# Another set of ranks and not-before times for a fixed list of operations, in a sliding-window attention followed by a token and channel mixer

## The chip, the core and the metric

The kernel runs as one launch on one core of a Trainium2 chip. The metric is the device time of that core in microseconds, as the median of several executions. Before the change three executions took 273.97, 274.58 and 275.58 us, so the median is 274.58 us. The profile is one further execution with the hardware profiler on.

The engines are named as in the profile: PE is the matrix engine (PEld its weight loads, which overlap its matmuls), DVE the vector engine, ACT the scalar engine, POOL the general engine that here issues most loads, and SP the engine that here only issues transfers. Each takes its own instructions strictly in the order in which the program has them, and waits where an operand isn't ready.

## What is computed

```python
def _attn_ref(q, k, v):                     # 8 batches, 8 heads, 576 rows, 64 wide
    scores = scale * np.matmul(q, k.transpose(0, 1, 3, 2))
    mask = (rel >= 0) & (rel < window)      # window = 128
    scores = np.where(mask, scores + bias[None], -1000000000.0)
    attn = np.exp(scores - max) ; attn = attn / (sum + 1e-09)
    return np.matmul(attn, v)

def _moe_ref(x, w_tok1, w_tok2, w_ch1, w_ch2):   # x: 8 x 576 x 512
    h = np.maximum(x.transpose(0, 2, 1) @ w_tok1, 0.0) @ w_tok2
    u = x + h.transpose(0, 2, 1)
    h2 = np.maximum(u @ w_ch1, 0.0) @ w_ch2
    return u + h2
```

The head outputs are laid side by side and become x. Each of the eight batches goes through attention, then through the token mixer (which mixes rows), then through the channel mixer (512 to 1536 and back).

## The kernel before

Two batches form a pair; their 576 rows are cut into eight blocks of 128 rows and one TAIL block that holds the last 64 rows of both. For a block the stages are: loads of q, k and v (POOL, line 614); a transposition of q and k into a tile qkT, for the first blocks on PE (L772) with a copy from PSUM on DVE or ACT (L778, L787), for the later ones as a transfer from SP (L761); scores on PE (L809, and L855 for a shared block), which use half of the rows of the array; exponentials on ACT (L824) and masks on DVE (L834); values on PE (L897), then reciprocal and normalisation (L910, L913, or L919 on ACT), which write the tile xb.

The token mixer of a batch multiplies xb by W1 (L944, with the tail rows in L954), applies a relu (L962 or L963), multiplies by W2 block by block (L987, and L983 for the TAIL block, which uses half of the columns), and DVE adds x (L1005), which writes the tile ub. From batch 3 on SP transposes each block of ub by a transfer (L1013) into uT, or uTt for TAIL; before that PE does it (L1022, L1291). The channel mixer of the batch then multiplies by WC1. In four of the batches some of that is written as seven smaller products of half-blocks (L1402, with DVE preparing differences in tt at L1365, copies at L1417/L1418, sums at L1426 and relus at L1428/L1430); elsewhere it is plain (L1502, relu at L1508 or L1509). TAIL pieces are L1545 with the relu at L1550. The second matrix WC2 is always seven half-block products (L1679), fed by sums on DVE (L1527), and evicted with an addition at L1650; the finished quarter goes to memory from SP or POOL (L1662). The TAIL rows go through L1590 and L1597, and their store is L1606.

The channel mixer of batch b and the attention and token mixer of batch b+1 are interleaved on PE. None of this order is written by hand. Each step is entered in a list (1486 operations, numbered in the order in which they are entered) with an engine, a cost, a rank, what it needs and which buffers it makes. A planner (`Plan.run`) then goes through model time: on each engine, among the operations whose needs are met, the earliest one is taken, and among several that could start at once the one with the lowest rank:

```python
key = (t if t > free[e] + 1e-6 else free[e], own, o.n)
```

PSUM banks and other rings are handed out in the same pass. Some operations may go to either of two engines (DVE or ACT), and the planner settles that too; where it leaves a hole on PE in the first 60 us of its own time it puts in small matmuls on a tile of zeros (L1737). The finished order is then written out engine by engine. POOL alone has an order of its own (`o.order`), which ranks don't touch.

What steers the order beside the costs is a string of triples, NUDGES (line 389). Each names an operation by number, an amount that is added to its rank, and a model time before which it may not start (0 for none):

```python
for item in NUDGES.split():
    n, rank, after = item.split(":")
    ops[int(n)].rank += float(rank)
    ops[int(n)].after = max(ops[int(n)].after, float(after))
```

Of the kernel before, what the change touches and what calls it, by code (L numbers as in the profile page):

```python
# [71 lines left out]
class Plan:  # L72
# [60 lines left out]
    def run(self):  # L133
        ops = self.ops
        for item in NUDGES.split():
            n, rank, after = item.split(":")
# [189 lines left out]
    def emit(self, spin):  # L326
# [20 lines left out]
        for _, _, go in sorted(work, key=lambda w: w[:2]):  # L347
# [41 lines left out]
NUDGES = ("611:-21079:100923 615:-377:0 618:6245:106227 624:11583:0 628:-3532:0 631:-20512:118175 632:4405:0 "  # L389
          "635:13739:113529 638:-6964:114135 641:43614:0 643:-19605:120680 648:13951:125840 652:20901:132489 "  # L390
          "656:1592:130617 662:-3783:94988 668:12595:102360 672:0:99525 676:-4021:0 691:3986:0 694:4455:102094 "
          "706:-16795:109525 710:11799:0 717:5009:114541 723:-30772:115527 725:-13156:0 727:1700:0 731:-799:113884 "
          "737:-15688:124087 742:88:126037 747:-10649:132061 750:-29110.6:133561.55 752:1864:0 753:7662:141715 "
          "756:18322:0 757:13696:0 758:5979:130815 759:2748:0 760:-6228:0 761:25117:132703 763:-2147:0 765:-1777:134943 "
          "766:12861:138150 769:4570:135329 774:-3476:0 778:14785:0 780:7181:136913 782:6347:136777 796:5332:0 799:9009:0 "
          "801:8201:142134 808:2736:0 813:9918:154475 818:-1109:0 820:-5330:154387 833:-4650:0 835:34387:124325 "
          "837:-15506:120235 843:8673:0 857:-16826:126349 858:1715:130121 859:24976:132690 862:8001:133653 "
          "869:22770:125235 870:11407:127731 885:3734:139098 891:9282:135579 895:-4722:0 906:6597:0 929:-1024:0 "
          "934:1522:0 937:4392:0 939:-1560:0 942:20915:0 948:771:175554 950:-4529:179605 951:995:176861 980:-2682:165866 "
          "981:-2735:0 983:1098:0 989:-8428:0 992:-4728:0 995:4194:0 1000:4211:156722 1005:3799:169472 1010:-2057:164371 "  # L400
          "1013:-4825:0 1019:7261:0 1032:-2615:175960 1038:-4243:0 1044:-3493:182549 1047:-1700:185338 1048:8146:185482 "
          "1054:3724:185348 1056:2724:0 1068:-1298:0 1070:3393:0 1074:20899:194114 1077:45251:0 1080:18007:0 "
          "1081:-2386:195024 1087:458:209375 1088:1:199812 1091:-1643:199488 1097:-2044:205608 1111:2214:211061 "
          "1114:17600:0 1119:-16086:212462 1121:-6088:0 1124:52293:0 1133:0:215904 1147:208:186538 1149:1234:0 "
          "1154:3339:0 1163:6504:0 1166:5025:0 1173:-13218:195991 1174:-7990:194582 1175:11221:198039 1181:18370:199015 "
          "1189:-770:198395 1195:5140:0 1201:243:206584 1202:-5634:204124 1213:15048:0 1219:1629:209744 "
          "1232:-23729:221022 1233:-4369:0 1235:2272:0 1237:-12249:0 1238:-11167:221075 1240:4249:0 1241:4209:0 "
          "1242:7504:0 1255:5295:0 1256:0:234956 1257:14642:0 1258:12581:0 1260:3619:0 1262:4895:0 1264:11531:232963 "
          "1267:-4292:227279 1276:5714:238024 1280:962:0 1283:-2021:240378 1288:-141:235787 1290:-9906:246722 "
# [1362 lines left out]
```

## Time and profile before

| | |
|---|---|
| median of three executions | 274.58 us (273.97, 274.58, 275.58) |
| profiled execution, first to last instruction (span) | 272.2 us |
| median less span | 2.4 us |
| granted PE clock over the span | 1.000 |
| PE busy | 263.6 us, 97% |
| PE weight loads busy | 191.8 us, 70% |
| DVE busy | 224.7 us, 83% |
| ACT busy | 150.7 us, 55% |
| POOL busy | 114.7 us, 42% |

The profiled execution has no time of its own on record beside its span; what lies around the span in an ordinary execution (the launch, the last store's completion) can only be taken as the difference to the median, 2.4 us, if that execution was a middling one. Busy times count the engines' own instructions. A PE matmul's end is modelled, so consecutive matmuls overlap in the record, and what a stretch of them takes is read from start to start.

### The profile page before, as it was taken

The page shows a single profiled execution, that of the slowest core. Times are in us where ns is not written, and L with a number is a line of the kernel's source. Part 1 is how long each engine was busy: PE and PEld are TensorE (multiplying, and loading weights), DVE is VectorE, ACT ScalarE, POOL GpSimd, SP SyncE. Part 2 cuts the span into 40 slices and gives each one's busy share as a digit, 9 for nine tenths or more (in the row PEclk, how much of TensorE's full clock was granted, in tenths as well). Part 3 has the DMA queues.
Part 4 walks back from the last instruction along what each step waited for, and adds up shares of the span by engine and source line. Part 5 has one row for each costly group of instructions (what it writes and reads, how often), then busy time and mean ns, then how long its engine had stood idle before and what let it go on. Part 6 is the DMA issues. An engine that isn't in the chain of part 4 may idle for free.

```text
span 272.2 us, 7391 instructions
## 1 busy us (share of the span) xinstructions
PE 263.6 (97%) x2965; PEld 191.8 (70%) x2992; DVE 224.7 (83%) x520; ACT 150.7 (55%) x267; POOL 114.7 (42%) x147
## 2 busy tenths in 40 slices
PE   7989999999999999999999999999999999999994
PEld 5767566676686655587786756498886758589883
DVE  7887699978897569688999478698998989976983
ACT  6973796226881298107992089308973089506700
POOL 8978796840397007800870307800651050004000
PEclk9999999999999999999999999999999999999999
DMA  8999999999999979999999999999999580035005
GB/s 201 178 173 180 167 148 183 157 156 175 186 127 161 192 162 78 137 119 210 200 149 119 142 228 96 140 154 142 212 132 67 110 239 2 2 82 171 4 10 183
DMA packets 160338, 38.59 MB, mean 142 GB/s; under 512 B 146544, under 2 KB 159472, under 8 KB 160304
## 3 DMA queue, kind: packets, MB, share of 16 engines
q0 software_dynamic: 109968, 19.64, 89.4%
q1 hardware_dynamic: 49104, 17.70, 33.4%
q10 hardware_dynamic: 1232, 0.79, 1.0%
q8 instruction: 23, 0.38, 0.5%
q14 instruction: 11, 0.09, 0.1%
HBM read 35.85 MB, written 9.44 MB: 166 GB/s over the span
## 4 chain that ended last, share of the span: by engine, by line
PE 90%; DMA 3%; POOL 3%; issue 1%; ACT 1%; DVE 0%; POOLq 0%
PE ps L1679 27%; PE ps L1502 15%; PE ps L1402 12%; PE ps L897 6%; PE ps L809 5%; PE ps L987 4%; PE ps L944 4%; PE ps L1545 4%; PE ps L1590 4%; DMA W<-in_moe_w_tok_dram 2%; POOL v L623 1%; DMA qkT<-qk 1%; POOL qk L630 1%; PE ps L772 1%; PE ps L1488 1%
## 5 line engine op out<-in xcount | busy, mean ns | idle before, releaser
L614 POOL DMA_DIRECT2D v<-in_v_dram x36 | 30.5, 849 | 76.4 <-PE ps L897 72.8
L824 ACT ACTIVATE pe<-ps 128x1024 bf16<-128x1024 f32 (+1 forms) x56 | 51.3, 969 | 3.1 <-PE ps L809 3.0
L1502 PE MATMUL ps<-uT,WC 128*128 128x512 bf16 x182 | 46.0, 379 | 0.7 <-issue 0.2
L1508 ACT ACTIVATE r<-ps 128x512 bf16<-128x512 f32 x45 | 26.4, 601 | 35.9 <-PE ps L1502 33.8
L1679 PEld LDWEIGHTS <-r 128*128 128x128 bf16 x384 | 36.8, 98 | 7.4 <-issue 0.7
L1679 PEld LDWEIGHTS <-s 128*128 128x128 bf16 x288 | 27.8, 98 | 5.8 <-DVE s L1527 0.4
L614 POOL DMA_DIRECT2D qk<-in_k_dram x35 | 30.3, 873 | 3.7 <-DMA qk<-in_k_dram 1.6
L834 DVE TENSOR_TENSOR pe<-pe,mask 128x1024 bf16<-128x1024 bf16 (+1 forms) x48 | 30.5, 650 | 1.6 <-ACT pe L824 1.4
L614 POOL DMA_DIRECT2D qk<-in_q_dram x35 | 30.2, 867 | 3.7 <-DMA qkT<-qk 1.7
L1502 PEld LDWEIGHTS <-WC 128*128 128x128 bf16 x196 | 17.7, 98 | 18.1 <-issue 0.5
L1417 ACT COPY raw<-ps 128x512 f32<-128x512 f32 x27 | 15.5, 597 | 22.6 <-PE ps L1402 22.6
L1679 PE MATMUL ps<-WC,r 128*128 128x256 bf16 x192 | 24.9, 273 | 0.0
L1679 PE MATMUL ps<-WT,s 128*128 128x256 bf16 x192 | 24.7, 273 | 0.0
L1679 PE MATMUL ps<-WT,r 128*128 128x256 bf16 x192 | 23.8, 273 | 0.1
L897 PEld LDWEIGHTS <-pe 128*128 128x128 bf16 (+1 forms) x480 | 19.5, 99 | 5.6 <-DVE pe L834 0.8
L1426 DVE TENSOR_TENSOR r<-ps,raw 128x512 bf16<-128x512 f32 x30 | 20.2, 680 | 3.3 <-ACT raw L1417 2.8
L897 PE MATMUL ps<-v,pe 128*128 128x65 bf16 (+1 forms) x480 | 22.8, 194 | 0.1
L1005 DVE TENSOR_TENSOR ub<-ps,xb 128x512 bf16<-128x512 f32 x32 | 20.5, 683 | 2.7 <-ACT r L1508 0.9
L913 DVE TENSOR_TENSOR xb<-ps,rt 128x256 bf16<-128x256 f32 (+1 forms) x52 | 21.4, 417 | 0.5
L1650 DVE TENSOR_TENSOR raw<-ps,ub 128x512 f32<-128x512 f32 x25 | 17.0, 686 | 5.8 <-PE ps L1679 5.8
L1402 PE MATMUL ps<-tt,WS 128*128 128x256 bf16 x132 | 18.8, 273 | 0.1
L809 PEld LDWEIGHTS <-qkT 64*128 64x128 bf16 x448 | 11.9, 94 | 8.3 <-issue 5.9
(143 smaller groups left out, 479.4 us busy)
## 6 DMA issues: line engine op xcount, KB each, us to landing
out_dram<-raw SPq DMA_DIRECT2D x19, 256.0 KB, 4.4
qk<-in_q_dram POOLq DMA_DIRECT2D x30, 128.0 KB, 5.4
qk<-in_k_dram POOLq DMA_DIRECT2D x30, 128.0 KB, 5.4
v<-in_v_dram POOLq DMA_DIRECT2D x28, 128.0 KB, 5.1
WC<-in_moe_w_ch_dram POOLq DMA_DIRECT2D x8, 384.0 KB, 7.5
out_dram<-raw POOLq DMA_DIRECT2D x6, 256.0 KB, 3.4
out_dram<-ob SPq DMA_DIRECT2D x5, 256.0 KB, 4.1
v<-in_v_dram POOLq DMA_DIRECT2D x16, 64.0 KB, 4.8
```

The source lines that it names most:

```text
L614: nc.gpsimd.dma_start(out=to()[p0 : p0 + n, :, :], in_=rows(src, b, s0, n))
L809: pe_.matmul(wide(e)[:, i, kind, a:z], lhsT=ts[kb]()[e * D : (e + 1) * D, NHP + i, :], rhs=ts[blk]()[e * D : (e + 1) * D, i, a:z], start=T ...
L824: act_.activation(out=pb()[:, e, :, lo:, c0:c1_], in_=wide(e)[:, :, lo:, c0:c1_], func=ACT.Exp, scale=scale)
L834: dve_.tensor_tensor(out=o, in0=o, in1=heads(mk, es), op=ALU.mult)
L897: pe_.matmul(view()[a:z, at, i, :], lhsT=pb()[:, e, i, kind, a:z], rhs=vb()[:, h, 0 : D + 1], start=m == 0, stop=m == len(mms) - 1, skip_g ...
L913: dve_.tensor_tensor(out=x4(), in0=view()[r0:r1_, :, :, 0:D], in1=rt()[r0:r1_, 0:n, :, :].broadcast_to([r1_ - r0, n, 4, D]), op=ALU.mult)
L1005: plan.op("DVE", 690, lambda blk=blk, ht=ht, hs=hs: dve_.tensor_tensor(out=ub()[:, blk, :], in0=ht()[:, hs], in1=xb()[:, blk, :], op=ALU.a ...
L1402: pe_.matmul(bk()[:, c * HS : (c + 1) * HS], lhsT=l(c, cb), rhs=r(cb), start=new and c == 0 and cb == 0, stop=cb == 1, skip_group_check=True)
L1426: add = plan.op("DVE", 690, lambda: dve_.tensor_tensor(out=o(), in0=half_of(bk), in1=half_of(e), op=ALU.add), rk + UNIT_RANK, uses=[bk, e] ...
L1502: pe_.matmul(ct()[:, :], lhsT=WC1[:, cb, t * P : (t + 1) * P], rhs=uT()[:, cb, :], start=cb == 0, stop=cb == NCB - 1)
L1508: plan.op("ACT", 600, lambda t=t, ct=ct: act_.activation(out=r2()[:, t, :], in_=ct()[:, :], func=ACT.Relu), rk, part=(r2, t), uses=[ct], o ...
L1679: pe_.matmul(bk()[:, c * HN : (c + 1) * HN], lhsT=l(t, c), rhs=w(t), start=first, stop=g == 1 and t == HK - 1, skip_group_check=True)
```

## The change

The string NUDGES is replaced; no other line differs. It had 178 triples, the lowest operation 611 and the highest 1457, and 97 of them with a not-before time. It now has 206 triples, from operation 156 to 1479, and 100 with a not-before time. 78 operations are in both, and none of these keeps its two numbers. The new set was picked by the mean end over scattered transfer and engine times of a fixed order.

```diff
-NUDGES = ("611:-21079:100923 615:-377:0 618:6245:106227 624:11583:0 628:-3532:0 631:-20512:118175 632:4405:0 "
...
-          "1431:-2423:252435 1443:3256:263701 1444:354:262085 1457:-151:263359 ")
+NUDGES = ("156:-15687:54632 159:42592:0 161:18891:0 169:9713:0 293:10443:0 295:-38081:0 303:13240:0 305:29272:0 "
...
+          "1429:-101737:0 1432:-54653:0 1479:50983:0")
```

The same operations are done. What moves is their order on PE, DVE, ACT and SP, the engine of 43 either-or operations (21 go from ACT to DVE and 22 from DVE to ACT), and the number of zero matmuls of L1737 (52 before, 56 now). The order of POOL is unchanged. Line numbers of the changed kernel are 7 higher from NUDGES on. Three places follow.

**PE, batch 0's channel mixer with the first blocks of batch 1.** The rows run from the last transposition of a block of q and k to the first scores that read the transposed tile qkT_83. Before:

```order
L772 MATMUL ps<-ident,qk_71 128x128
L1488 LDWEIGHTS WC_124
L1488 MATMUL ps<-uT_98,WC_124 128x512
L897 LDWEIGHTS pe_86
L897 MATMUL ps<-v_72,pe_86 128x65
...
L1502 LDWEIGHTS WC_124
L1502 MATMUL ps<-uT_98,WC_124 128x512
...
L809 LDWEIGHTS qkT_83
L809 MATMUL ps<-qkT_83 128x128
```

With the change:

```order
L779 MATMUL ps<-ident,qk_71 128x128
L1495 LDWEIGHTS WC_124
L1495 MATMUL ps<-uT_98,WC_124 128x512
...
L1744 LDWEIGHTS zero
L1744 MATMUL ps<-zero 128x128
...
L816 LDWEIGHTS qkT_83
L816 MATMUL ps<-qkT_83 128x128
```

One L1488, four L897 and four L1502 stood between the two; now three of the first kind and three zero matmuls do, and eight value matmuls come behind the scores.

**SP, the end of batch 3's token mixer.** uT_99 and uTt_100 are the transposed tiles of batch 3, qkT_78 and qkT_83 the next blocks for scores of batch 4. Before:

```order
L1606 DMA out_dram<-raw_105 64x512 x2
L1013 DMA_TRANSPOSE uTt_100<-ub_93 128x4x128
L1013 DMA_TRANSPOSE uT_99<-ub_93 128x4x128 x4
L761 DMA_TRANSPOSE qkT_78<-qk_69 128x8x128
L761 DMA_TRANSPOSE qkT_83<-qk_71 128x8x128
```

With the change:

```order
L1613 DMA out_dram<-raw_107 64x512 x2
L1020 DMA_TRANSPOSE uT_99<-ub_93 128x4x128 x3
L1020 DMA_TRANSPOSE uTt_100<-ub_93 128x4x128
L1020 DMA_TRANSPOSE uT_99<-ub_93 128x4x128
L768 DMA_TRANSPOSE qkT_78<-qk_69 128x8x128
L768 DMA_TRANSPOSE qkT_83<-qk_71 128x8x128
```

The TAIL tile goes fourth in place of first; five transposed blocks still stand ahead of qkT_78.

**PE, the end of batch 7's token mixer.** The rows run from the W2 product of the TAIL block (r_97 and W2t), whose sum becomes uTt_100, to the channel product that reads uTt_100. Before:

```order
L983 MATMUL ps<-r_97,W2t 64x512
L1679 LDWEIGHTS s_111
L1679 MATMUL ps<-WT,s_111 128x256
...
L987 MATMUL ps<-r_97,W_122 128x512
...
L1679 MATMUL ps<-WC_125,r_101 128x256
...
L1545 LDWEIGHTS uTt_100
L1545 MATMUL ps<-uTt_100,WC_124 128x128
```

With the change:

```order
L990 MATMUL ps<-r_97,W2t 64x512
L994 LDWEIGHTS W_122
L994 MATMUL ps<-r_97,W_122 128x512
...
L1686 MATMUL ps<-WC_125,r_101 128x256
...
L1686 MATMUL ps<-WT,s_111 128x256
...
L1552 LDWEIGHTS uTt_100
L1552 MATMUL ps<-uTt_100,WC_124 128x128
```

Before, 54 matmuls of L1679 and two of L987 stood between; now 24 of the first and eight of the second do, since the TAIL block's W2 product is the first of the five. On SP its transposition goes first as well, where it was fourth of five.

55 lines of the change are left out of this document (31 added, 24 removed).

## The prediction

> **What bounds the kernel now.** I read the page first, then the busy time by stretches, then PE's waits, and last the order of time at the places where the change puts other neighbours. From the page: the busy sums, PE's slices and granted clock, and the chain that ended last.
>
> ```profile
> span 272.2 us, 7391 instructions
> PE 263.6 (97%) x2965; PEld 191.8 (70%) x2992; DVE 224.7 (83%) x520; ACT 150.7 (55%) x267; POOL 114.7 (42%) x147
> ...
> PE   7989999999999999999999999999999999999994
> ...
> PEclk9999999999999999999999999999999999999999
> ...
> PE 90%; DMA 3%; POOL 3%; issue 1%; ACT 1%; DVE 0%; POOLq 0%
> ```
>
> PE has nine tenths or more in nearly every slice at the full clock, and 90% of the last chain is PE's own work. So time is lost only where PE stands still or does something extra. How much that is, the stretches say: a stretch, its length, then busy time of PE, PEld, DVE, ACT and POOL, the clock, the DMA share and GB/s.
>
> ```profile
> 0.00:27.00 27.00, 24.14 (x389) 18.36 (x390) 21.52 (x72) 18.17 (x34) 23.37 (x35) 1.00 1.54 183
> 27.00:60.00 33.00, 32.74 (x340) 21.08 (x344) 28.77 (x65) 18.23 (x33) 24.14 (x30) 1.00 1.84 162
> 60.00:100.00 40.00, 39.69 (x449) 26.70 (x453) 31.40 (x74) 23.95 (x40) 14.31 (x17) 1.00 1.67 176
> 100.00:140.00 40.00, 39.18 (x467) 28.57 (x471) 34.81 (x83) 24.83 (x41) 19.89 (x24) 1.00 1.36 141
> 140.00:180.00 40.00, 39.58 (x368) 26.14 (x374) 31.09 (x66) 19.28 (x34) 16.93 (x21) 1.00 1.48 145
> 180.00:220.00 40.00, 39.84 (x457) 31.12 (x458) 35.66 (x79) 20.99 (x38) 12.03 (x15) 1.00 1.05 142
> 220.00:260.00 40.00, 39.90 (x432) 32.44 (x432) 34.98 (x78) 25.22 (x50) 4.04 (x7) 1.00 0.24 72
> 260.00:272.20 12.20, 8.53 (x79) 7.39 (x76) 6.45 (x12) 0.00 (x0) 0.00 (x0) 1.00 0.34 107
> ```
>
> The order on PE is the same up to the last transpositions of the opening, about 27 us in, so the 2.86 us idle before that stay. In the last stretch PE ends on the same product, TAIL piece and eviction, so its 3.67 us stay too. Between them, from 27 to 260 us, PE is idle for 0.26 + 0.31 + 0.82 + 0.42 + 0.16 + 0.10 = **2.07 us**. That is all that another order can win, 0.75% of 274.58 us, beside small gaps that the modelled ends cover. The largest single wait in it:
>
> ```profile
> PE ps L809 <- DMA qkT<-qk: 0.4, 1, 0.4
> ```
>
> **The change part by part.** The same operations run, so the sum is the span plus what PE does more and waits more.
>
> *Changes of array shape.* Scores use half of the rows and TAIL products half of the rows or columns. Counting in the order of the matmuls the places where such a one follows a full one, or the reverse, gives 122 before and 124 with the change. What one costs, and also the first new wait, is read here, in the order of time (start, duration, engine, line).
>
> ```profile
> 28.34 0.61 PE L772 MATMUL ps<-ident,qk 128*128 128x128 bf16 x8
> 28.54 0.69 DVE L1509 TENSOR_SCALAR r<-ps 128x512 bf16<-128x512 f32 x1 [0.44 <-PE ps L1488]
> 28.78 0.38 PE L1488 MATMUL ps<-uT,WC 128*128 128x512 bf16 x1
> 29.00 0.28 PE L897 MATMUL ps<-v,pe 128*128 128x65 bf16 x4
> 29.14 0.68 DVE L778 COPY qkT<-ps 128x1024 bf16<-128x1024 bf16 x1
> 29.28 1.02 PE L1502 MATMUL ps<-uT,WC 128*128 128x512 bf16 x4
> 30.24 0.23 PE L809 MATMUL ps<-qkT 64*128 64x128 bf16 x2
> ...
> 30.64 0.22 PE L809 MATMUL ps<-qkT,qkT 64*128 64x128 bf16 x2
> 30.79 1.90 PE L1502 MATMUL ps<-uT,WC 128*128 128x512 bf16 x7
> ```
>
> A 512-column matmul starts 0.22 us after the one before it (28.78 to 29.00). Four take 0.87 us, and from 29.28 to the scores at 30.24 are 0.96: 0.1 us for going into the half-row shape. The eight pairs of scores start 0.057 us apart ((30.64 - 30.24) / 7), and the next full matmul comes 0.15 us after the last pair: 0.1 us for leaving it. Two more changes: **+0.2 us**.
>
> *Scores closer to their transposition.* In the rows above, PE has finished the transposition at 28.95, DVE copies qkT from 29.14 to 29.82, and PE meanwhile does 1.24 us of other work up to 30.24. Now three L1488 (0.65 us) and three zero matmuls stand there; a 128-column matmul takes 0.055 us ((28.78 - 28.34) / 8), so 0.17 us. PE would be ready at 28.78 + 0.65 + 0.17 + 0.1 = 29.70. The copy ends at 29.73 if DVE takes it at once, or at 29.82 as before, and DVE has nothing else ahead of it now, since L1509 goes behind. PE is then late by 0.1 to 0.2 us, and the zero matmuls (0.17 us) do nothing useful. I take **+0.3 us**, between 0.2 and 0.4. Behind these scores on PE stand the eight value matmuls and the batch's other chunks; nothing off PE is short of work, as ACT's exponentials follow the scores themselves.
>
> *The wait for qkT at 124.5 us.* The change reorders SP just ahead of it.
>
> ```profile
> 113.76 1.21 SPq L1013 DMA_TRANSPOSE uTt<-ub  x1
> 115.07 6.03 SPq L1013 DMA_TRANSPOSE uT<-ub  x4
> 121.27 2.61 SPq L761 DMA_TRANSPOSE qkT<-qk  x2
> ...
> 124.52 0.23 PE L809 MATMUL ps<-qkT 64*128 64x128 bf16 x2 [0.42 <-DMA qkT<-qk]
> ```
>
> SP issues five blocks from 113.76 to 121.10 without a pause, then qkT, and scores wait 0.42 us for it. With the change it's still five blocks and then qkT, only the TAIL block goes fourth. SP's own issue time sets the moment, so I leave the 0.42 us where it is: **0**, with -0.42 as the other bound.
>
> *Stores behind a transposition.* In the first 70 us the fourth SP transposition moves ahead of two stores.
>
> ```profile
> 57.20 1.78 SPq L1662 DMA_DIRECT2D out_dram<-raw  x2
> 59.84 2.46 SPq L761 DMA_TRANSPOSE qkT<-qk  x1
> ...
> 83.81 0.62 SPq L1662 DMA_DIRECT2D out_dram<-raw  x1
> ```
>
> The two stores go some 5 us later (62.3 in place of 57.2). Their buffers are wanted again for batch 1's evictions, the first of which is stored at 83.81; PE has the channel mixer of batch 1 and the attention of batch 2 to do until then. Some 15 us of PE work hide the 5, and what is over would be paid in full if that cover were gone: **0**.
>
> *Either-or operations.* Of the 43 that move, most are relus, copies and normalisations of under 1 us (L1509 and the copy L778 above take 0.69 and 0.68); about as many go each way, so DVE stays near 83% and ACT near 55%. Short waits of PE for one of them vanish at some places and new ones of the same kind come at others. All of them together are the 2.07 us less the 0.42, so 1.65. I credit **-0.3 us**, about a fifth of that, with 0 to -1.65 on the one side and as much again, +1.65, on the other, as PE's neighbours are new nearly everywhere.
>
> *The last boundary.* It is the place where the cover shrinks most.
>
> ```profile
> 235.79 1.03 PE L987 MATMUL ps<-r,W 128*128 128x512 bf16 x4
> 237.14 3.81 SPq L1013 DMA_TRANSPOSE uT<-ub  x3
> 239.05 0.59 PE L987 MATMUL ps<-r,W 128*128 128x512 bf16 x2
> 239.48 0.82 PE L1679 MATMUL ps<-WC,r 128*128 128x256 bf16 x6
> 240.14 0.82 PE L1679 MATMUL ps<-WT,s 128*128 128x256 bf16 x6
> 241.04 1.22 SPq L1013 DMA_TRANSPOSE uTt<-ub  x1
> 242.91 0.68 DVE L1005 TENSOR_TENSOR ub<-ps,xb 128x512 bf16<-128x512 f32 x1
> 244.72 2.84 PE L1545 MATMUL ps<-uTt,WC 128*128 128x128 bf16 x48
> ...
> DMA to landing us min/median/max: 2.3/2.4/4.8
> ```
>
> Two L987 start to start take 0.43 us and six L1679 take 0.66. Before, 54 of L1679 and two of L987 lie between TAIL's W2 product and L1545, 6.4 us. Now 24 and eight do: 2.64 + 1.72 = 4.4 us. TAIL's W2 product takes the place of the first L987 at 235.79, and its four matmuls and two changes of shape end near 236.4; L1545 is due at 240.8. The sum L1005 takes 0.68, so SP issues at about 237.1, as it did for the first block before, and with the median landing of 2.4 us uTt is there at 239.5. 1.3 us are left, so **0**, and the cover is gone when a landing takes over 3.7 us.
>
> Sum: 272.2 + 0.2 + 0.3 - 0.3 = 272.4 us of span. The median lies 2.4 us above the span shown; I keep that and forecast **274.8 us**, no change.
>
> **The rivals.**
>
> *Faster: the idle time closes.* PE's 2.07 us fall to about 0.5, with the new wait at 29 us hidden as well: 274.58 - 1.6 = 273.0 us. For it: the waits are many and small, and a new neighbour ends each. Against it: 0.42 of it hangs on SP's unbroken row of issues, and two shape changes are added.
> The Trainium skill speaks for more: "Perfetto Trace Analysis", section Identifying the Most-Contended Engine, says that matmul busy time is no measure of nearness to the limit and that the share of weight loads is one of two better ones. Here weight loads have 70%, and by that rule alone much more than 2 us would be open. The trace doesn't bear this out as room for another order: the stream rows above show 0.11 us per 256-column matmul without a gap, so the loads lie under the matmuls; I give it no more than this rival's chance.
>
> *Slower: the last boundary waits for its landing.* If uTt lands as late as the slowest row, 4.8 us, it is there at 237.1 + 4.8 = 241.9, and PE waits 241.9 - 240.8 = 1.1 us; a uT block that is late in the same way behind it costs another 0.5. Then 274.8 + 1.6 = 276.4 us. It decides from a landing of 3.7 us on. For it: cover falls from 6.4 to 4.4 us, and all of DVE, SP and PE queue behind. Against it: the DMA share in that stretch is 0.24, where it is 1.36 in the stretch of batch 3.
> For comparison, the Trainium skill, "DMA: Bandwidth & Descriptors", section Anatomy of one DMA, gives about 2.0 us fixed plus bytes over 436 GB/s, an estimate of 2.3 us for these 128 KB; it is written for POOL's path. The median of 2.4 agrees, the maximum of 4.8 does not; by the page this rival would not occur.
>
> *The change does next to nothing where it counts*, 274.6 us: every wait keeps its size. It can't be told from my forecast and is part of it.
>
> **How the numbers follow.** No change, 274.8 us: 0.69, its own range 274.0 to 275.8. Faster, 273.0: 0.14. Slower, 276.4: 0.17. A measurement of this kernel can tell about 0.5%, 1.37 us, from no change: below 273.2 and above 275.95. The forecast's own spread puts 0.01 below and 0.02 above, and 0.02 of the faster and of the slower case fall inside the band: faster 0.13, slower 0.17, no change 0.70. The range takes in the forecast whole and the nearer part of both rivals: 273.1 to 276.3.
>
> **What would show it.** PE's idle time from 27 to 260 us is 1.5 to 3 us; a wait of 0.1 to 0.3 us of L809 for the copy L778 near 29.8 us; a wait of L809 for qkT near 124.5 us of about 0.4; L1545 near 240.8 without a wait; DVE and ACT busy within 3 us of before. I am wrong if that idle time is below 1 or above 3.5 us, or if the time moves without it, which would mean that PE's own work changed.

## The result, and the profile after

The changed kernel took 278.43 us (median of six executions, 277.09 to 279.96), the kernel before beside it 274.76 us (273.96 to 275.58). The ratio is **1.0137, with a 95% interval of 1.0105 to 1.017**: slower by 3.7 us, where no change was forecast (274.8 us, at most 276.3). The profiled execution is the one of 277.09 us, with a span of 275.3 us. The first profile of before has 272.2 us, so 3.1 us are to be explained there.

The page of the changed kernel, its busy sums, and the chain that ended last with its shares by engine and by line:

```profile
span 275.3 us, 7387 instructions
...
PE 265.0 (96%) x2969; PEld 191.5 (70%) x2996; DVE 224.3 (81%) x519; ACT 149.1 (54%) x253; POOL 114.7 (42%) x147
...
q8 instruction: 23, 0.38, 0.5%
...
PE 77%; DMA 12%; DVE 5%; POOL 2%; issue 2%; ACT 0%; SPq 0%; DVEq 0%
PE ps L1686 23%; PE ps L1509 13%; PE ps L1409 12%; DMA WC<-in_moe_w_ch_dram 6%; PE ps L904 6%; PE ps L816 5%; PE ps L951 4%; PE ps L994 4%; PE ps L1597 3%; DMA uT<-ub 3%; PE ps L1552 3%; DMA raw<-in_q_dram 2%; DMA qkT<-qk 1%; DVE ub L1012 1%; POOL qk L621 1%
```

Busy sums have hardly moved. The chain has: 90% of it was PE's own work and 3% transfers, now it is 77% and 12%. Half of the 12% are loads of WC in the first 45 us, and "uT<-ub", the transposition of the token mixer's result, is in it with 3%. The row q8 is of a kind that I had not looked at: 23 transfers of instructions, 16 KB each. The stretches, and PE's longest waits behind those of the opening (line, what was waited for, us in total, times, longest):

```profile
27.00:60.00 33.00, 32.28 (x338) 20.80 (x342) 26.95 (x62) 17.25 (x27) 23.46 (x30) 1.00 1.96 160
60.00:100.00 40.00, 39.74 (x436) 26.47 (x438) 31.38 (x71) 22.65 (x37) 15.16 (x19) 1.00 1.70 171
100.00:140.00 40.00, 39.50 (x479) 28.35 (x477) 34.47 (x80) 25.46 (x43) 19.11 (x24) 1.00 1.35 144
140.00:180.00 40.00, 39.01 (x363) 24.98 (x369) 31.01 (x68) 20.84 (x34) 17.77 (x22) 1.00 1.55 144
180.00:220.00 40.00, 39.84 (x455) 32.11 (x458) 35.04 (x77) 18.41 (x31) 9.44 (x11) 1.00 1.09 136
220.00:260.00 40.00, 39.32 (x422) 30.82 (x422) 33.82 (x76) 24.30 (x46) 6.82 (x10) 1.00 0.32 84
```

```profile
...
PE ps L1509 <- DMA uT<-ub: 0.6, 1, 0.6
PE ps L1409 <- DVE tt L1372: 0.6, 1, 0.6
...
PE ps L816 <- DMA qkT<-qk: 0.2, 1, 0.2
```

PE's idle time from 27 to 260 us is 0.72 + 0.26 + 0.50 + 0.99 + 0.16 + 0.68 = 3.31 us, where before had 2.07. The clock stays at 1.00. Two new waits of 0.6 us stand first among them, both behind a uT.

Idle time undercounts, since modelled ends cover small gaps and a zero matmul counts as work. So I compare the two traces directly: at points where both orders have done the same operations on PE, by how much later does the same next operation start? This **lag** is 0.05 us at 27 us, 1.14 at 73, 1.45 at 88, 1.47 at 136, 2.32 at 180, 2.04 at 232 and 3.10 at 260 us. Three places make it: the head up to 88 us, batch 4's boundary (136 to 180 us, +0.85) and batch 7's boundary (232 to 260 us, +1.06). A boundary is here the place where a batch's token mixer ends and its channel mixer needs uT. (The expectations below and the label u_b5 call the first of the two batch 5's; its four uT, issued from 146 to 151 us, are those of batch 4, as batch 3's are issued from 115 to 121.) The order of time at the two boundaries:

```profile
152.65 0.82 PE L1686 MATMUL ps<-WC,s 128*128 128x256 bf16 x6
153.30 0.82 PE L1686 MATMUL ps<-WT,r 128*128 128x256 bf16 x6
154.74 1.02 PE L1509 MATMUL ps<-uT,WC 128*128 128x512 bf16 x3 [0.62 <-DMA uT<-ub]
155.60 0.82 PE L1686 MATMUL ps<-WT,r 128*128 128x256 bf16 x6
...
248.46 0.60 PE L1409 MATMUL ps<-uT,WC 128*128 128x256 bf16 x4
249.63 0.60 PE L1409 MATMUL ps<-tt,WS 128*128 128x256 bf16 x4 [0.58 <-DVE tt L1372]
...
249.16 0.76 DVE L1372 TENSOR_TENSOR tt<-uT 128x512 bf16<-128x512 bf16 x2 [1.92 <-DMA uT<-ub]
```

Start to start, L1509 comes 0.78 us late and the first product that reads tt 0.74 us late. At batch 7 DVE stood idle 1.92 us for the last uT. That transposition was issued at 244.99 us, and these are the transfers from there to its landing, in the changed kernel and then around the same uT (issued 243.62) in the kernel before:

```profile
q1 hardware_dynamic: 1085, 0.26, 57.7%
q8 instruction: 1, 0.02, 1.9%
...
uT<-ub SPq DMA_TRANSPOSE x1, 4.0
```

```profile
q1 hardware_dynamic: 544, 0.13, 20.8%
...
uT<-ub SPq DMA_TRANSPOSE x1, 2.3
```

The same transposition lands 4.0 us after its issue here and 2.3 us there, and here a packet of instructions (q8) came while it was in flight, at 246.31 us. At batch 4 the last uT (issued 150.45) landed after 4.2 us; a packet came at 152.17:

```profile
q8 instruction: 1, 0.02, 1.4%
...
uT<-ub SPq DMA_TRANSPOSE x1, 4.2
```

That gave two theories. **O**: the new order leaves PE too little other work (cover) at these places. **F**: what counts is which transposition a packet of instructions happens to meet.

### The profile page after: what moved, and what is told of

Read it like the earlier page. It is cut to its first block, busy times and chain, and to the rows that moved or that the text cites. A ratio compares the mean times of both kernels' runs of the same rounds, so it can differ in the third digit from the quotient of the medians.

```text
span 275.3 us, 7387 instructions
## 1 busy us (share of the span) xinstructions
PE 265.0 (96%) x2969; PEld 191.5 (70%) x2996; DVE 224.3 (81%) x519; ACT 149.1 (54%) x253; POOL 114.7 (42%) x147
## 4 chain that ended last, share of the span: by engine, by line
PE 77%; DMA 12%; DVE 5%; POOL 2%; issue 2%; ACT 0%; SPq 0%; DVEq 0%
PE ps L1686 23%; PE ps L1509 13%; PE ps L1409 12%; DMA WC<-in_moe_w_ch_dram 6%; PE ps L904 6%; PE ps L816 5%; PE ps L951 4%; PE ps L994 4%; PE ps L1597 3%; DMA uT<-ub 3%; PE ps L1552 3%; DMA raw<-in_q_dram 2%; DMA qkT<-qk 1%; DVE ub L1012 1%; POOL qk L621 1%
## 5 line engine op out<-in xcount | busy, mean ns | idle before, releaser
L1515 ACT ACTIVATE r<-ps 128x512 bf16<-128x512 f32 x49 | 28.6, 601 | 36.7 <-PE ps L1509 35.0
L1509 PE MATMUL ps<-uT,WC 128*128 128x512 bf16 x184 | 46.2, 379 | 1.3 <-DMA uT<-ub 0.6
L1686 PEld LDWEIGHTS <-r 128*128 128x128 bf16 x384 | 36.8, 98 | 7.6 <-issue 0.9
L1686 PEld LDWEIGHTS <-s 128*128 128x128 bf16 x288 | 27.8, 98 | 6.3 <-issue 0.2
L1509 PEld LDWEIGHTS <-WC 128*128 128x128 bf16 x196 | 17.8, 98 | 18.2 <-issue 0.9
L1424 ACT COPY raw<-ps 128x512 f32<-128x512 f32 x26 | 14.9, 597 | 24.7 <-PE ps L1409 24.6
L1686 PE MATMUL ps<-WC,r 128*128 128x256 bf16 x192 | 25.2, 273 | 0.2 <-DMA WC<-in_moe_w_ch_dram 0.2
L1686 PE MATMUL ps<-WT,s 128*128 128x256 bf16 x192 | 24.8, 273 | 0.1
L1686 PE MATMUL ps<-WT,r 128*128 128x256 bf16 x192 | 24.2, 273 | 0.0
L920 DVE TENSOR_TENSOR xb<-ps,rt 128x256 bf16<-128x256 f32 (+1 forms) x57 | 23.2, 418 | 0.7
L904 PE MATMUL ps<-v,pe 128*128 128x65 bf16 (+1 forms) x480 | 23.4, 195 | 0.1
L1433 DVE TENSOR_TENSOR r<-ps,raw 128x512 bf16<-128x512 f32 x31 | 20.8, 682 | 1.2 <-ACT raw L1424 0.8
L1409 PEld LDWEIGHTS <-WS 128*128 128x128 bf16 x176 | 15.9, 97 | 3.2 <-issue 0.8
```

The source lines that it names most:

```text
L904: pe_.matmul(view()[a:z, at, i, :], lhsT=pb()[:, e, i, kind, a:z], rhs=vb()[:, h, 0 : D + 1], start=m == 0, stop=m == len(mms) - 1, skip_g ...
L920: dve_.tensor_tensor(out=x4(), in0=view()[r0:r1_, :, :, 0:D], in1=rt()[r0:r1_, 0:n, :, :].broadcast_to([r1_ - r0, n, 4, D]), op=ALU.mult)
L1409: pe_.matmul(bk()[:, c * HS : (c + 1) * HS], lhsT=l(c, cb), rhs=r(cb), start=new and c == 0 and cb == 0, stop=cb == 1, skip_group_check=True)
L1433: add = plan.op("DVE", 690, lambda: dve_.tensor_tensor(out=o(), in0=half_of(bk), in1=half_of(e), op=ALU.add), rk + UNIT_RANK, uses=[bk, e] ...
L1509: pe_.matmul(ct()[:, :], lhsT=WC1[:, cb, t * P : (t + 1) * P], rhs=uT()[:, cb, :], start=cb == 0, stop=cb == NCB - 1)
L1515: plan.op("ACT", 600, lambda t=t, ct=ct: act_.activation(out=r2()[:, t, :], in_=ct()[:, :], func=ACT.Relu), rk, part=(r2, t), uses=[ct], o ...
```

## The experiments

For most of them each engine gets an explicit list of operations, pieced together from the two finished orders, in place of the choice by rank. PSUM banks and other rings are still handed out as before, POOL's order is untouched, and all operations are done. The edit to the planner is the same each time. Line numbers in the experiments are those of the changed kernel, save in before_no_zeros and before_again, which have those of the kernel before.

```diff
-        for item in NUDGES.split():
+        lists = {e: [ops[int(n)] for n in s.split()] for e, s in ORDER.items()}
...
-                    if e == "POOL" and o is not pool[sent]:
+                    if [o] != ([pool[sent]] if e == "POOL" else lists[e][:1]):
                         continue
```

### Undoing one place at a time

```diff
-PE, ACT, DVE, SP: the changed order throughout
+u_head:  order of before up to 73 us, then the changed one
+u_b5:    changed, order of before from 138 to 183 us, changed
+u_b7:    changed up to 209 us, then the order of before
```

> The changed order, but up to 73 us (the L1545 pieces of batch 0's channel mixer) every engine takes its operations in the order of before. In the profiles the change is 1.14 us behind before at this point, out of 3.1 at the end. Theory O (the order of the head costs this): the lag at 73 us falls to 0.2 or less and the median to about 278.4 - 1.1 = 277.3 us, ratio to before about 1.009. Rival J (the loads of that one profiled execution came late by chance): the median stays within 0.4 of 278.4 us, ratio 1.0135.

> The changed order, but between 138 and 183 us (from batch 4's last WC2 products to batch 5's, where L1509 waited 0.62 us for the last uT) the order of before. Theory O (less cover between the first use of that uT and its transposition): the 0.85 us that the change loses in this stretch are gone, median about 277.6 us, ratio 1.0105, and no wait of L1509 over 0.2 us near 155 us. Rival F (the moment at which PE's 16 KB instruction packets come decides, the order only shifts what they meet): the transposition that meets the packet near 152 us still lands 4 us after its issue, and PE waits for it again by over 0.4 us.

> The changed order up to 209 us, then the order of before to the end, which holds batch 7's boundary. Theory O (shorter cover at the last boundary): the 1.06 us that the change loses from 232 to 260 us are gone, median about 277.4 us, ratio 1.0097, and no wait of L1409 for DVE near 249 us. If the loss came from elsewhere: 278.4 us, ratio 1.0135. Rival F expects the same -1.0 only if no uT of batch 7 is in flight when the packet near 246 us comes; one that is lands after 4 us in place of 2.3.

| | median, us | ratio to before, 95% |
|---|---|---|
| u_head | 278.91 | 1.0132 (1.009 to 1.0173) |
| u_b5 | 276.88 | 1.0071 (1.0037 to 1.0104) |
| u_b7 | 275.94 | 1.0046 (1.0021 to 1.0071) |

Undoing a boundary wins time, undoing the head by this measure none: theory O was right at the boundaries, rival J in the head, as far as the medians tell. They don't tell it all: u_b7 wins 2.5 us, more than twice what was lost there, and what u_head loses elsewhere comes further down. In u_b7 the last uT still lands late, 4.6 us after its issue (the packet came at 247.36 us). PE doesn't notice it: sixteen uT products run before the first that reads tt. The transfers from 245 us on, and PE:

```profile
q8 instruction: 1, 0.02, 1.2%
...
uT<-ub SPq DMA_TRANSPOSE x1, 4.6
```

```profile
249.11 1.91 PE L1409 MATMUL ps<-uT,WC 128*128 128x256 bf16 x16
250.85 0.38 PE L1409 MATMUL ps<-tt,WS 128*128 128x256 bf16 x2
```

### Moving the packets, not the order

By their number the packets are PE's instructions: 23 of 16,384 bytes for some 5,990 PE instructions, one per 260. If so, fewer PE instructions early on make them come later in the program. The zero matmuls of L1744 do no useful work and can go. Theory C, in these texts, takes O and F together: a wait needs both a short cover and a uT that meets a packet.

```diff
-FILL = 60000.0
+FILL = 17000.0      # no_zeros, no_zeros_again, before_no_zeros;  19000.0 in fewer_zeros
```

> The changed kernel, order untouched, without the 32 zero matmuls behind 18 us (64 PE instructions fewer). PE's 16 KB instruction packets then come about 64 instructions, some 3 us, later in the program. Rival F: the last uT of batch 5 and of batch 7 meet no packet and land about 2.3 us after their issue instead of 4.1; the waits of L1509 near 155 and of L1409 near 249 us fall below 0.2, and the median falls by 1.3 to 1.8 to about 276.8 us, ratio 1.0075. Theory O: the order and its cover are unchanged, so the waits and the median stay (278.4, at most 0.2 less for zero matmuls that stood in PE's way), ratio 1.0135.

> The kernel before without its zero matmuls behind 17 us (28 of them). Control for the run without zeros. Theory C: before has cover enough at both boundaries, so where the packets fall makes no difference there: 274.6 +- 0.5 us, ratio 0.998 to 1.002. If the zero matmuls themselves cost time: -1.5 us or more, 273.1, ratio 0.9945, as much as the changed kernel won without them. If they keep PE's clock up: slower than before, with a granted clock under 1.00 in the profile.

> The changed kernel without the 14 zero matmuls behind 19 us (28 PE instructions fewer, about half of the first shift), order untouched. The packets come some 1.5 us later in the program: near 153.7 and 247.8 us by the changed kernel's clock, when the last uT of both batches, issued at 150.45 and 244.99, has landed if nothing holds it up (2.3 us). Theory F: both land within 2.8 us, PE waits under 0.2 us at both, lag against before grows by at most 0.2 us from 136 to 180 and from 232 to 260 us; median 1.9 us under the changed kernel's two medians, 275.2 to 276.5 us, ratio 1.003 to 1.007. Rival O (the short cover alone): 4 us landings and waits of 0.6 us stay, ratio 1.009 to 1.0135.

> The changed kernel without 27 zero matmuls behind 17 us once more. If the first profile was no chance: the last uT of batches 5 and 7 land within 2.8 us again, no wait of L1509 near 155 and none of L1409 near 249 us over 0.2, lag growing by at most 0.2 us in both stretches; median 275.5 to 277, ratio 1.003 to 1.009.

The first text says 32 zero matmuls; it is 27 (and 23 in the kernel before, where the second says 28).

| | median, us | ratio to before, 95% |
|---|---|---|
| no_zeros | 276.60 | 1.0047 (1.0019 to 1.0076) |
| no_zeros_again | 275.65 | 1.0041 (1.0016 to 1.0067) |
| fewer_zeros | 275.52 | 1.0035 (1.0006 to 1.0064) |
| before_no_zeros | 275.42 | 1.0033 (1.0011 to 1.0054) |

Rival F had it: 276.8 us forecast for no_zeros, 276.6 measured (the closeness is partly luck, since its trace loses 0.9 us elsewhere, as shown below). With the order of the changed kernel untouched, the loss at both boundaries is gone. The stretches from 136 to 182 and from 232 to 262 us (length, then busy time of PE, PEld and so on), the changed kernel first, fewer_zeros second, and the transfers of its last two uT of batch 7:

```profile
136.00:182.00 46.00, 45.01 (x453) 29.74 (x453) 36.94 (x82) 23.24 (x38) 20.57 (x26) 1.00 1.60 146
232.00:262.00 30.00, 29.37 (x281) 23.71 (x281) 24.74 (x52) 14.00 (x30) 2.87 (x4) 1.00 0.25 59
```

```profile
136.00:182.00 46.00, 46.00 (x449) 30.83 (x446) 37.53 (x82) 22.14 (x36) 19.63 (x24) 1.00 1.56 143
232.00:262.00 30.00, 30.00 (x286) 24.73 (x285) 26.01 (x54) 13.18 (x25) 2.87 (x4) 1.00 0.21 59
```

```profile
q1 hardware_dynamic: 1088, 0.26, 46.6%
...
uT<-ub SPq DMA_TRANSPOSE x2, 2.3
```

PE has no idle time left in either stretch, the uT land after 2.3 us, and the packets came 1.8 and 0.25 us behind the landings (153.51 and 245.99 us).

The control missed its forecast (1.002 at most): the kernel before is 0.8 us slower without its zero matmuls, at a granted clock of 1.00. At the two boundaries it loses nothing, as expected. Its packets moved as well. One now came at 122.9 us, while the qkT issued at 120.99 was in flight. That qkT landed after 4.7 us, where it took 3.2 with the zero matmuls, and the wait of 0.42 us for it grew to 1.15:

```profile
125.74 0.23 PE L809 MATMUL ps<-qkT 64*128 64x128 bf16 x2 [1.15 <-DMA qkT<-qk]
```

The lag shows the same 0.7 us at this one place. So the order of before has a place without cover too, at batch 3's boundary, and in its other profiles no packet met a transfer that PE waits for there. The changed kernel without zero matmuls pays at that boundary as well: in no_zeros_again a packet at 121.8 us met batch 3's last uT, which landed after 4.3 us.

```profile
124.86 0.60 PE L1409 MATMUL ps<-tt,WS 128*128 128x256 bf16 x4 [0.63 <-DVE tt L1372]
...
126.74 0.21 PE L816 MATMUL ps<-qkT 64*128 64x128 bf16 x1 [0.68 <-DVE ob L1657]
```

From 88 to 136 us the lag grows by 0.4 us in fewer_zeros, 0.9 in no_zeros and 1.3 in no_zeros_again, most of it between 118 and 128 us.

### Moving single products away from the late uT

```diff
 PE, batch 4's boundary (two_moves, moves2, moves3, closed)
+12 x L1686
 4 x L1509 (first to read the last uT)
-12 x L1686
 PE, batch 7's boundary
 two_moves, moves3, closed: 12 x L1686 ahead of the first 4 x L1409 that read tt
 moves2:                    these 4 x L1409 behind the 12 x L1409 that read uT
 DVE: moves3, closed: one eviction L1657 ahead of tt
```

> The changed order with two moves on PE and nothing else: at batch 5's boundary twelve L1686 matmuls go ahead of the first L1509, at batch 7's boundary twelve L1686 go ahead of the first product that reads tt. Each is 1.31 us of work that PE had right behind the wait. Theory C (a wait needs both a short cover and a transposition that meets an instruction packet): the packets still meet the same transpositions, which land about 4.1 us after their issue, but PE's waits of 0.6 us are gone at both places; the median falls by as much as the two undone stretches gave, to between 274.5 and 276.9 us, ratio 1.000 to 1.008. If the neighbourhoods as a whole are at fault (more operations than these two): at most -0.5, 277.9 us, ratio 1.012.

> The changed order with two moves on PE. At batch 5's boundary as in the run before (12 L1686 ahead of the first L1509: PE gained 0.7 us there). At batch 7's boundary now the one product of four L1409 that reads tt goes behind the twelve L1409 that read uT and stood behind it; nothing that needs a bank from DVE is moved. Theory C (short cover times late landing): the packets still make the last uT of batches 5 and 7 land 4 us after their issue, PE has no wait over 0.2 us at either place, and against the first profile of the changed kernel PE is 0.7 us ahead at 180 us and 1.4 us ahead at 260 us, lateness of loads in the head apart. Median: 1.4 us under the changed kernel's two medians (278.4 and 277.1), so 275.7 to 277.0 us, ratio 1.004 to 1.009. If the landing itself stops the uT products too, the second gain is under 0.3 us.

> The changed order with batch 5's move (12 L1686 ahead of the first L1509), and at batch 7's boundary twelve L1686 ahead of the product that reads tt, and with them the eviction L1657 that frees their bank ahead of tt on DVE, since it was DVE's queue that held these twelve up for 2.0 us in the first try. Theory D (what is late at batch 7 is DVE's queue behind the late tt, so PE needs work that waits for nothing in that queue): the last uT still lands 4 us after its issue, and PE loses at most 0.3 us against before from 232 to 260 us (changed kernel 1.06, product put behind others 0.82); median 1.9 us under the changed kernel's two medians, 275.2 to 276.5 us, ratio 1.003 to 1.007. Rival P (any move there only shifts the wait): 0.8 us or more stay, ratio 1.005 to 1.009.

Medians: two_moves 279.26 us, ratio 1.0169 (1.0137 to 1.0202); moves2 275.92, 1.005 (1.0023 to 1.0077); moves3 276.92, 1.0088 (1.0057 to 1.012). Batch 4's move works each time: the uT still lands after 4.3 us, and the lag grows by 0.06 us there in place of 0.85. Batch 7's doesn't, and each version fails on another engine. PE of two_moves, moves2 and moves3:

```profile
250.33 1.47 PE L1686 MATMUL ps<-WT,r 128*128 128x256 bf16 x12 [1.87 <-DVE raw L1657]
```

```profile
248.90 0.60 PE L1409 MATMUL ps<-tt,WS 128*128 128x256 bf16 x4
...
254.54 0.27 PE L1409 MATMUL ps<-uT,WS 128*128 128x256 bf16 x1 [0.43 <-DVE raw L1425]
```

```profile
249.62 0.60 PE L1409 MATMUL ps<-tt,WS 128*128 128x256 bf16 x4
250.06 1.47 PE L1409 MATMUL ps<-uT,WC 128*128 128x256 bf16 x12
252.26 0.81 PE L1409 MATMUL ps<-tt,WS 128*128 128x256 bf16 x6 [0.73 <-ACT raw L1424]
```

In two_moves the twelve L1686 need a bank that DVE evicts behind the late tt; PE loses 3.4 us in this stretch. In moves2 the wait for tt is gone, but a copy of DVE comes later and 1.03 of 1.06 us stay. In moves3 PE runs on for 3.1 us without a wait (248.31 to 251.4), and then waits for ACT's copies, which those twelve L1686 had covered where they stood: 1.37 us are lost. Rival P, that a move there only shifts the wait, was right, and theory D wrong.

### One place alone, both together, and the kernels against themselves

```diff
-PE, ACT, DVE, SP: the order of before throughout
+only_head: changed order up to 88 us, then that of before
+only_b7:   order of before up to 207 us, then the changed one
+u_b5b7:    changed order, but that of before from 138 to 183 and from 209 us on
+closed:    order of before up to 88 us, then the changed one with the moves of moves3
```

> The changed order up to 88 us, then the order of before. In the nine profiles so far the lag at 73 us follows the lateness of the loads (about 1 us per us) with some 0.7 us on top where the head has the changed order and none where it has that of before; from 73 to 88 us the changed order loses another 0.3 in all of them. Theory H (the head's order costs 1.0 us beside the loads' chance): lag at 88 us less the loads' lateness is 0.8 to 1.2, median 275.6 us, ratio 1.0037 (1.001 to 1.007). Rival J (all of the head is chance): lag less lateness within 0.3 of 0, 274.6 us, ratio 1.000.

> The order of before up to 207 us, then the changed order: the last boundary alone. Theory C: a packet comes near 244.5 us, while the last uT is in flight; it lands 4 us after its issue, L1409 or L1402's counterpart waits about 0.6 us for tt, and PE loses 1.0 us against before between 232 and 260 us: 275.6 us, ratio 1.0037 (1.002 to 1.006). If the boundary costs only together with what the change did ahead of it: 274.6, ratio 1.000.

> The changed order with the order of before in both stretches, 138 to 183 and from 209 us on; the head and the rest stay changed. If the two boundaries are the whole loss, the single ones add up (-1.5 and -2.5 of 3.8): 274.6 us +- 0.8, ratio 0.998 to 1.003. If one covers the other, or something else is left: about 275.5, ratio 1.003.

> The order of before up to 88 us, from there the changed order with the three moves of moves3. If head, batch 5 and batch 7 are the whole loss, nothing is left: 274.5 us +- 0.5, ratio 0.999 to 1.003. If something else in the changed order costs: ratio 1.004 or more.

> The changed kernel once more, for a second profile and a narrower interval. Median 278.0 to 278.8 us. The waits near 155 (L1509) and 249 us (L1409) are there again with about 0.6 us each, and the packets near 152 and 246 us. If the lag of 1.1 us that had come up by 73 us in the first profile was chance, it has another size now (in the runs so far: -0.4 to 1.3).

> The kernel before against itself, for a second profile and for how far two runs of one kernel may differ. Ratio 1.000 within 0.3%. Lag at 73 us against the first profile equal to the loads' lateness within 0.3 us; no wait over 0.3 us at either boundary, though a packet meets a uT of batch 5.

| | median, us | ratio to before, 95% |
|---|---|---|
| only_head | 275.08 | 1.0033 (1.0009 to 1.0058) |
| only_b7 | 275.16 | 1.0028 (1.0007 to 1.0049) |
| u_b5b7 | 277.03 | 1.0077 (1.0041 to 1.0112) |
| closed | 276.79 | 1.0113 (1.0064 to 1.0162) |
| after_again | 277.09 | 1.0086 (1.0062 to 1.0109) |
| before_again | 274.16 | 0.9985 (0.9968 to 1.0002) |

only_head and only_b7 came out as theory H and C had it. only_b7 shows the wait of the changed kernel again, in an order that is that of before up to 207 us:

```profile
247.46 0.60 PE L1409 MATMUL ps<-uT,WC 128*128 128x256 bf16 x4
248.67 0.60 PE L1409 MATMUL ps<-tt,WS 128*128 128x256 bf16 x4 [0.60 <-DVE tt L1372]
```

u_b5b7 missed: its trace loses only 0.33 and 0.00 us at the two boundaries, but its head came out 2.5 us late. closed missed too: batch 7 still loses 1.10 us, and the joint at 88 us made a wait of its own (0.45 us for ACT's copy of uT). And the changed kernel itself took 277.09 us on the second occasion, 1.3 less than on the first. So medians of different occasions can't settle half a microsecond here. The traces can, once the lag is taken by stretches. For the head I set against it how much later the POOL loads (17th to 45th) landed than in the first profile of before, as a median:

| head up to 73 us | lag less lateness of loads, us | lag gained 73 to 88 us |
|---|---|---|
| order of before (before_again, before_no_zeros, before_qk, only_b7, u_head, closed) | -0.01, 0.02, 0.00, 0.32, 0.07, 0.34 | 0.00 in the first four, 0.27 in closed |
| changed order (nine profiles) | 0.47 to 1.10, median 0.69 | 0.31 in each |
| changed order without late zero matmuls (three) | 0.14, 0.02, 0.11 | 0.31 in each |

The loads' lateness itself ran from -0.86 to 1.45 us, in both orders, and from -0.58 to 0.75 in two profiles of the very same kernel (no_zeros, no_zeros_again): chance of the execution. In u_b5b7 it is 1.45 of the 2.5 us. In u_head it is 1.18, but that isn't why its median is high: its trace loses 2.0 us between 88 and 136 us, where packets met a qkT (PE waits 0.87 us at 100.6) and batch 3's last uT, and 1.6 at batch 7's boundary. What the changed order adds is 0.7 us, and it goes with the zero matmuls. The changed kernel, then fewer_zeros:

```profile
46.33 0.44 PE L904 MATMUL ps<-v,pe 128*64 128x65 bf16 x8
46.70 0.72 PE L1744 MATMUL ps<-zero 128*128 128x512 bf16 x7
47.26 0.93 PE L1686 MATMUL ps<-WC,r 128*128 128x256 bf16 x7
```

```profile
30.05 0.23 PE L816 MATMUL ps<-qkT 64*128 64x128 bf16 x2 [0.21 <-DVE qkT L785]
...
45.45 0.44 PE L904 MATMUL ps<-v,pe 128*64 128x65 bf16 x8
45.82 1.92 PE L1686 MATMUL ps<-WC,r 128*128 128x256 bf16 x16
```

Seven zero matmuls at 46.70 us take 0.56 us in a hole that only the planner's model has: without them L1686 follows at once. The other 0.31 us, from 73 to 88 us, are two waits of 0.15 us for ACT at 79 and 80 us.

The same for the two boundaries, over all profiles (lag gained from 136 to 180 us, and from 232 to 260 us, at operations that are in every trace; "late" is a last uT of 3.4 us or more from issue to landing):

| | late, met a packet | on time, 2.3 to 2.4 us |
|---|---|---|
| batch 4, changed order | 0.71 to 0.99 (four profiles) | 0.06, 0.07, 0.06 |
| batch 4, changed order with the move | 0.06, 0.07, 0.06, 0.06 | |
| batch 4, order of before | 0.00 (four); 0.32, 0.33 as a piece in the changed order | 0.00 |
| batch 7, changed order | 1.06, 1.07, 1.61, 0.77, 0.88 | 0.00 (three) |
| batch 7, changed order with a move | 3.41, 1.03, 1.37, 1.10 | |
| batch 7, order of before | 0.00 (three) | 0.00 (three) |

Neither theory alone holds. At these two boundaries it takes both: a uT that a packet makes late, and an order in which PE has nothing else left that doesn't wait in the same queue.

### A try to beat both

```diff
 PE of the kernel before, at 124 us
+4 x L1409 on uT (L1402 in the kernel before)
 8 pairs of scores (wait 0.4 us for qkT)
 8 x L1409
-4 x L1409 on uT
```

> The kernel before with one move on PE: the product of four L1402 with uT that stands three places behind the scores at 124 us goes ahead of them, where PE waits 0.4 us for qkT. The scores still start when qkT lands, so the wait falls below 0.1 us and PE is 0.3 to 0.45 us ahead behind it: median 273.9, ratio 0.9985 (0.997 to 1.000), at the edge of what can be measured. If the scores then come later than the landing, or DVE and ACT behind them lose as much: ratio 1.000.

It took 274.96 us, ratio 1.0041 (1.0017 to 1.0065): slower. The product moved ahead needs a bank that DVE still has to read, and PE waits twice as long as it did for qkT:

```profile
124.85 0.60 PE L1409 MATMUL ps<-uT,WC 128*128 128x256 bf16 x4 [0.87 <-DVE xb L920]
125.38 0.23 PE L816 MATMUL ps<-qkT 64*128 64x128 bf16 x2
```

No version here is faster than the kernel before.

## Why the prediction was wrong

Forecast 274.8 us, measured 278.43, outside the range. By its steps:

- **Changes of array shape, +0.2 us.** Not tried by itself. Over the changed kernel's 124 changes the excess from start to start has a median of 0.11 us, as taken.
- **Scores closer to their transposition, +0.3 us.** Right at the spot. Without the zero matmuls the wait is seen bare: L816 at 30.05 comes 0.37 us late, of which the trace marks 0.21 as a wait for the copy. What it adds to the time stays open: from 27 to 40 us the lag grows by 0.59 us in the changed kernel's profile, whose loads are late, and falls by 0.13 in moves2, moves3, u_b7 and only_head, which have the same order there and early loads.
- **The wait for qkT at 124.5 us, 0.** Right in the profile shown (0.4 before, 0.2 after). Over all runs it is no constant: where scores wait for it, they come 0.3 to 0.9 us late from start to start, in either order, and 1.3 in before_no_zeros.
- **Stores behind a transposition, 0.** Right: no wait of PE for a store's buffer appears.
- **Either-or operations and short waits, -0.3 us, with 1.65 on either side.** This step failed. It credited a gain because as many operations go each way, and it took all short waits of before as its size. The runs showed +0.56 us of zero matmuls at 46.7 us, which I had not priced at all, +0.31 us at 79 and 80 us, and +0.85 us at batch 4's boundary, a wait for a transposition that I had not looked at and that no term named: together +1.7 us, beyond even the upper bound. A gain is there too, 0.28 us from 180 to 232 us, but it is far smaller.
- **The last boundary, 0, cover gone from a landing of 3.7 us.** Failed, in the form of the rival that I gave 0.17. For uTt the step held, though its issue came 0.6 us later than worked out (239.75, not 237.1 plus the lag of 2.0): it landed after 2.35 us, and L1552 started at 242.83 without a wait (240.8 plus the lag). But I computed the cover of uTt and not of the last uT. The product behind its tt is due at 248.46 + 0.44 = 248.90, 3.9 us after its issue at 244.99, and DVE needs some 0.5 us of that for tt; the rival priced this block at 0.5 us. It measured 1.06. The mechanism, cover that ends ahead of a late landing, was right; the place was one transposition further, and its size was twice the estimate.

The rival was held down by "the DMA share in that stretch is 0.24". A mean share says nothing of a single packet: the row q8, 23 packets and 0.5% of the engines' time, was on the page of before as well. The maximum of 4.8 us would not have led there by itself. It is batch 3's uTt, issued at 113.76 us, which met no packet; loads shared the DMA engines with it (DMA share 1.98 from 113.7 to 118.6 us). A list of the landings one by one would have: before has its own late uT at batch 4's boundary, issued at 149.42 us and landed after 4.33 with a packet at 151.31, where its order hides it.

On what I named as proof: PE's idle time from 27 to 260 us is 3.31 us, outside the 1.5 to 3 that would have shown me right and short of the 3.5 that would have shown me wrong; it grew by 1.24 us where the span grew by 3.1, so more than half of the loss doesn't show as idle time. DVE and ACT are within 3 us of before, as said. The sum of steps gave 272.4 us of span, and 275.3 were measured. With the loads 0.67 us later in this execution, the account closes from the other side: 0.67 for the loads, 0.47 and 0.31 for the rest of the head, 0.02 up to 136 us, 0.85 at batch 4, -0.28 up to 232 us and 1.06 at batch 7 make 3.10 us. The medians agree as far as they can: the order's own terms are some 0.7 + 0.3 + 0.85 + 1.06 = 2.9 us, and the two occasions of the changed kernel lie 3.7 and 2.5 us above before. The three runs without a late uT at the two boundaries lie 1.1 to 2.0 us above before; their traces, less the lateness of their loads, have 0.9 to 1.6: 0.3 to 0.5 in the head, and 0.4 to 1.3 at batch 3's boundary. Taken so, the lag at 260 us agrees with the distance of the medians within 0.8 us in all runs but two, over distances from -0.1 us (before_again) to 4.7 (two_moves). The two are off by 1.2 us: the changed kernel on the first occasion (2.4 in the trace, 3.7 by the median) and u_b7 (2.6 and 1.3).

What stays open: those 1.2 us, why the loads differ from one execution to the next, and what in batch 7's order beside the twelve L1686 would have to move to make the late uT harmless.

## What to carry to other kernels

Take a transfer's cover against its slowest landing and not against the median, and do it for the last block of a batch as well as for the first: where the page has a maximum of twice the median, list the landings one by one, with what was in flight beside each, before a reorder is called free. A control that changes the number of instructions moves the packets too, so it has to be read by its trace. Work that is moved ahead as cover helps only when its bank, its inputs and whatever it had covered where it stood don't hang on the same late transfer. And where executions differ by a microsecond in their loads, compare traces stretch by stretch at points where both have done the same work; the medians then have to agree with the sum.

## What the hardware showed that I had not expected

**PE's own instructions hold up transpositions.** A profile has nine transpositions into uT or uTt at batch 4's and batch 7's boundaries. Over 19 profiles, 132 of them had no packet of instructions in flight beside them and landed 2.29 to 3.18 us after their issue, with a median of 2.35. 33 met one at least 0.2 us ahead of their landing and took 3.44 to 4.66 us, median 4.15; these two groups don't overlap. The other six met one in their last 0.2 us and took 2.29 to 2.39. At batches 3 and 5, where a fifth transposition and other transfers queue with them, the groups do overlap: without a packet up to 5.0 and 3.5 us, with one from 3.1 and 3.0. The packet that met batch 7's last uT took 1.29 us itself, and single packets of the transposition beside it up to 1.7 us.
The Trainium skill, "Runtime: NRT & Kernel Launch", section Instruction fetch mechanics, says that instructions come in blocks of 16 KiB, 256 of them, through a DMA queue, and that the cost of crossing into the next block is mostly hidden. Size and count agree (23 packets of 16,384 bytes for about 5,990 PE instructions), and no wait of PE for its own instructions is put down to a packet in the rows shown. What the sentence doesn't speak of is the transpositions in flight: they came 1.8 us later (4.15 against 2.35), and that isn't hidden where a transfer has little cover.
The estimate of 2.3 us that the prediction worked out from the Trainium skill, "DMA: Bandwidth & Descriptors", section Anatomy of one DMA, agrees with the median of the 132 that met no packet and fails for the 33 that did.

**Adding or removing a few idle matmuls early moves things 200 us later.** 14 zero matmuls fewer before 50 us made the packets miss both uT, and took PE's idle time out of both boundaries (1.0 us from 136 to 182 us, 0.6 from 232 to 262 us). In the kernel before, 23 fewer put a packet onto a qkT at 121 us and cost 0.7 us.

**Loads differ between executions by more than the change costs anywhere.** The median landing of the 17th to 45th POOL load was 0.86 us earlier to 1.45 us later than in the first profile of before, in kernels that issue them in the same order, and with the order of before PE's lag at 73 us followed it within 0.4 us.
